# Attention and gated feed-forward on one core: 159 instead of 153 key blocks on VectorE, 12 more homes for hidden tiles, row chains interleaved, a new order

## The chip, the core and the metric

The kernel runs on one core of a Trainium2 chip. The core has five engines that run their own instruction queues in order and meet through semaphores: TensorE (PE, matmuls; its weight loads are listed apart as PEld), VectorE (DVE), ScalarE (ACT), GpSimd (POOL) and SyncE (SP), which here issues nearly all DMAs. Matmuls write to PSUM (eight banks of 128 partitions x 512 floats); everything else lives in SBUF. The metric is device time in microseconds of one execution; lower is better.

## The reference, cut to what matters

One input x of 2048 rows and 512 columns is normalised and goes into two branches whose results are added to x.

```python
xn = layernorm(x)                                   # 2048 x 512
# attention, 32 heads of 16
q, k, v = split(xn @ wqkv)                          # wqkv 512 x 1536
p = softmax(q @ k.T * 16 ** -0.5)                   # 32 x 2048 x 2048
a = (p @ v) @ wo
# gated feed-forward, 1792 hidden columns
gate, up = xn @ W_gate, xn @ W_up
h = where(gate > 0, gate, 0) * up
return x + a + h @ W_down
```

The exponentials are the large part: 32 x 2048 x 2048 of them.

## The kernel before, in words

**Attention.** The queries are cut into four blocks of 512 (c4 = 0 to 3), the heads into four groups of eight (gg), each group into two halves of four heads (ee). That makes 32 blocks in order of time; each goes over the 2048 keys in 16 key blocks of 128 (kt). For a key block and four heads, TensorE makes four score tiles of 128 keys x 512 queries. The array is cut into tiles of 64 rows x 32 columns: an operation uses one half of the 128 rows with four matmuls side by side, and the two halves work beside each other.

What happens to the scores is set by the table `QUAD_AT`, a line for each of the 32 blocks and a character for each key block:

- a dot: two units go to ScalarE. Each is one activation of 128 x 1024 (L1389) that reads two PSUM banks and writes exponentials to `ring`; there are two such pairs of banks, used in turn. Then one pair of value operations (8 matmuls) adds the key block's share to the block's output.
- a digit: the key block goes to VectorE, in `quad` (L1336). VectorE evicts each of the four score tiles with a bias as int16 (L1344, "d1"); read as bf16, these bits approximate the exponential. Two shifted copies of this pattern, `qa` and `qb`, with other shifts, even out the error. Each copy is made either by one VectorE instruction (L1363, 128 x 2048) or by two GpSimd instructions (L1359, 128 x 512 int32 each); bit 0 of the digit puts `qa` on GpSimd, bit 1 `qb`. All three patterns then go through the value matmuls: 3 x 8.

`QUAD_AT` has 153 digits before, so 359 key blocks and 718 activations are left to ScalarE. Four banks of pool `b` serve VectorE's scores, the value accumulations, the projections and the feed-forward in turn.

At the end of each block `normalise` evicts the output to `o_sb`, and takes the row sums through three small DMAs and a reciprocal (L1239) to `rb`; GpSimd multiplies (L1251, L1256). For the second half of the heads the result goes through `oT1` and four small DMAs (stream `pk`) into `oT`, which lies in `x_sb`.

**Feed-forward.** `glu(c4, ft)` (L1016) makes one hidden tile, 128 hidden columns x 512 rows: 16 matmuls for up, evicted by VectorE to `up_sb` (L1040), 16 for gate, and one VectorE instruction that gates and multiplies into a home in `hT` (L1044). There are 4 x 14 such tiles and `NHS` = 20 homes. Some tiles of the next query block are made together with this block's, to share a load of weights (`shared`).

**Rows.** `out_rows(c4, i)` (L1058) makes 128 output rows: a chain of 14 matmul pairs over the hidden tiles with `W_down` (in `Wd`, and in the homes of `Wk` and `Wv` when these are done), then four over the attention result with `wo`, and a VectorE addition of x (loaded into `xr_sb`, two slots) and a store. The rows of the last query block can't wait for its last heads: their first part is kept in fp32 in `xnT` (`resid(i)`, columns 0 to 1023 of part i, L1099) or, for two of them, stays in its bank. All matmuls of a chain are made to depend on all tiles of `reads`.

**The order.** The program makes a graph of 8248 operations, `Graph.op` collecting what each reads and writes. The order of all of them is not made when the program is built: it stands in the string `PLAN` as numbers, found beforehand by a search over a model of the engines, with the slot of each tile behind it. `Graph.run` reads it, adds the dependencies that come from the reuse of slots, and `Graph.emit` writes each engine's queue with the semaphore waits that are not already implied. The list `seq` gives the feed-forward's tiles and rows their places in the graph: all tiles of a query block, then its four row chains. `Pool` objects hand out the slots (`P_h` those of hidden tiles).

Of the kernel before, what the change touches and what calls it, by code (L numbers as in the profile page):

```python
# [14 lines left out]
ALU = mybir.AluOpType  # L15
# [28 lines left out]
ROW_AT = 20  # L44
XBANKS = (0, 1, 2, 3)
# [40 lines left out]
    "3...3..3..2..3..",  # L86
    "2...2..3..0..3..",
    "2...3..3..2..3..",
    "2...3..3..2..3..",
# [4 lines left out]
    "2...3..3..2..3..",  # L94
    "2...3..3..0..3..",
    "2...3..3..2..3..",
# [25 lines left out]
PLAN_OPS = 8248  # L122
PLAN = (
    "c-m!K1z;3M7v67n?{Wzd96~7)9Euky#fn1{v}hoK;8KbdcXx*Z#UWUc1S{?yij?ARg%p<nA>8f!Z)SJzHvEN<&E4+Ilka`+dvmFxr2dbKFK%6lf2^OxpPcvTGN*FSxG*2!#(Uzg@iI@fAXj{^<+x8@"
    "%6)Si-}BZZIh1?Wi;8boZof|$L0|XHm3{A9SJrLzy}8dF<9#T;*NnG~=Zyz+<6X!r<1XE12mQnqv4Rfy92EJAaiv>UfZpcj3mo26tqZQ$U$U%#_ciYGN&bQHBUf~J#l2=5&xoHaJB&+R@m)eUmxgY6"
    "1Mf<TVy*7=RX$=o=v_jrEyKoj@vvM?guuAZe1Kaql;**5!dTnG<bKeNI7+LmDA0wmjtHuEL0$U9ZE&$8Qryc8bEQY-YT!n=#1=+S<f4Xo@?W{UVg>|8pbR&RMXi6VU8KqKRjx=k#ie36ubayl(KlZZ"
    "Hkp@Zm}T5xJ)_w0XF*%xKB#iV=avr+x@m*ulCD_6H(%v;1K@*@uf*hc-3Kr$F6MW|ECM5~#yipxX1ho6K#?I4w=!QwxG%ZBoN;c4Gq+cx`6k)JEI2SPpBQc_9_EqpWxi+|cG5G(8XkzOFxxIx2)WG;"
    "v#>-|tRzVEh^;*em;WkE095*CSm<HqH|`M|cr09qT?N{VqVkBF%{%E!F2OyVSrjJo#C@^#5)-#ki(ELx!R42&{H1*&2Hxz52r$buahFFFHO%CC#9Q)JX4)?UB?Bn-@h~$EIv~rA8_Cs;WrYXK$Nit2"
    "M!^`XNhfIu!$pr-LS8yEID~)F1h<%6rs(#5!hPxRm9Y^lkGYG%5gr*R0~OLCGBU+!z=V64=^WYo$tfJMfyPTKzOG}v;bF$wOvcRc*~FY;Bv>(tiF*u~8(XJvKX15AfN<jhZuJo_&2ULV6kSIO6u07Z"
    "n^5&Yev|jYSj=N$RJvkR9J6dQw^K}4WnknQ2KJbTo4lwq%O)-%r<f?UuuDHk&%DjiSK&Se(yeb+R>Tduswg~lX?yeb(aF4Nkg+hqF8uHqwZ!ZoHmb)Pd?OPS5BUuDmX8s2!)cF~_zloVDiYqnivk~q"  # L130
    "nY1CwOy{3m@(zy-tptie8y<@zOv?m=nS1CyhNEu=B`7eOk-4-{f*<_M5>EDG7OrJlj3<qH<B}A0Uq6ShIT>w0_7VdV7WXDQb<H4KFK}%NhI8+iw?X?D-P<nA;$d8|bq!xzx2@%?Juea2d0J6Ycihz4"
    "iKpttb}qMXVl_42%G{@Q45=jhvlSWL=1(da;oV)g$rSi7X|g-_={ghMqMLJ*p}1~7rOW*c)nvS?_#*193-N&Jm2bY<vBgpM1wl8Rg-!aJs>hOTHhssvVvX}uy4D`TRBeJ=Dnik}C}X4+x2a?83x)z8"
    "P7M7D-$pVbhF-Mp(9NeUoO!Rm(9_&TEIgIe=U=4H*8F8n=~jp=p$ePY^|cgh5n-d%d3{m#82#JSWxiUqOr$1lsdSSV4fZs9w5f$mrt#t2l1_2~v;V<-Ua~WEtC}S<>(DK_7H`2Y3_dto2=#_e`(*Vt"
    "g9R+@W;o|D>5$AY83nqH+ATj!ijo4rE1_gF@^%OKB%gf8QYqHkoEu9rL-W|xonmNwAueE>v%JypMjKYVr8c%?2{)Cy)N9<j!4?E=hFLc`6E;RMR`D1WWsO<B25P)&-fH?P6*#ko0@_pi<kkdX=$0AY"
    "b-5+Vm{;o?c`)6VVKthH$2WqAMUB=5`+#hhw3ZGx!(`SvynFdD{aNE?a4o!<6(z;2ck1!(p?il87~_pKDf!TwTKRHY?HQuc1c<PXTbt^pKioTXnWmT_=C;>JnKGs*-f6>xf;lFcv!dN{GbE;9x6M>u"
    "tGxmi+^fa8t?L>ypru?bvh&uSabXVK-jem|O>Rzxu+2K$8f>l3FN?r5-n!Fl)?9I`7NeRin;X0Yo9|xdypb~dl5M=V+J(jQTxUwEcI)dZ+$){!Ga*kcp}qZ)f7yfok84w%BYZKC*;~J_!F>T9pD$Lg"
    "wKR=+qeb4{Dc*a8A$73TabdB#?_Tq~fZmp;6JjBm8p}iYu<YymJXI&NkD1(em|@|J+X7_G_r|e=PXlpp!?%=(#HU<JN3zp?4wWi>+}2KQ8>O0Xl~f(sUZ(aVEw7$1k1xLH;Kqe{xT0`h;%p~f+y@f="
    "#p_;p@l;sh|G&hSV$NGd7UwJG5s<F|7}p*}VZKms-w?tjWty|PhuKd*OpyhXdll~h=qn<#3DUrn>{8^QZP1{H!?fBMj-cq?QyE3E23c=Ev+<-S)iIUHH1ypZowzl}*=oWjam0RH`z&R)mpDwI*-m<l"
    "-F07|Ft;`PiA9;#$$+)7uNRn3de2=9BdmiRk7BV6Yy}`&q(#PxSMb=*&x}+UozfUkpjaJ1w?-jDoZ4;U)~S*uq%4Y&t;FXmw^OfTQ-I1BptV7t`zB_<CwadlFOM}``;H!TQ?!_AHAhZ!d{$sJG>=UO"
    "d1G(1JfA4^wjMd;d86r_>22g_Vaiy^I@dFhV5&6Ejjp4Z+@^aMF;t8<-d594yhLR-ck95_cb;iKjx_V)v%mzJUGsU*?d;;frr#{In(EdXI=L}cf7WRB=e`4Acp1*BBi%UrvQE+zZg1!O|IYQTpS{dx"  # L140
    "$|c2ys{fY|+}6kKyz0d?-RgE28MgEzPu+w6uRGfN0k;H!ZxG?BdGL$7?I$6yW7*dV?1#Dh3u@)c7oS1c(QXGk=cxuQ+j&6h-r^gM6#U;x*8FCdAKuy4dLFh;>zmGX?)#j=D_LNDBBJ|t@SUU^D|oNG"
    "M@eQ@eZ#68w``rwHXEfvi<LiPH*@+_yo0?-A76~WHm_}JMuA-z!_p~&aCK4lrdEM9=c{hTMrZa<ldK$CM^8M}NNqn`u~d7itaI<-d#ZGCdp^DL$d(S9+jf{4kHI>%GGj?J$jx(H&OFv==beibWBj$w"
    "78R@SS;vST>oWzj$$7kEnRwbf@3So{=Ky95OXf)@^Du9dvMExXS<|k0<X}IAlAVehW?Lud<{+jh7R`IfT(=$E8T`X+XIOfwdXXSEWS_y&1}vCIM1iOJ>_oTb3-hBKZYg`8#b$f-wtZ`&P<-0ME;qcN"
    "W?8gsJ#CF~)`xSjv$|!Ki4?1)n`5H)Lm1hi%mXT)q~c!=S2k+09pR?_e1xYyd9&$m`-j1)`nmT5Q!hmM7jusHsZ>W%itn>jbJnr5lwFbXR39v*5(Zx?Z`((whHU3H;p`pAQk}(k&-)al+T16Uzxcc&"
    "RfzZ(AKAh7nJ)KDNvYgVb!h87$m7PG<dye!D)1ho=wEzNXdB<`r}MtHl4=^TO)p;6<^2>uNeu~KRCV||_LpmkzZsDFzXwh@Kfi|x##s@lx~l4@OK6(^Csp@P!L#(5pL!pe@iZ&^#O;|ikDrJBIxmN5"
    "HyIw}rPmy8`iIeXaYL}@CCkXz)iBM;{=sc}|0W6mIT%9TF{GhwRDQm6LOGnKJ#hi`S>=^LuFA(Mvz@dGeWyQ22CA=YyP#~k7n$CqnbBT%{vHFAOSuPp9hmHNyRHGnpJhl1czXvZ@+yt?%5lBqEqc@K"
    "@_R-$`0WU;wk3kD(v2yNW0SWbxDXIBDo1;b7GB<w?bB-Q9d#?VO&GuTs1t4fJ`RoPZvgPB*F*%hUk^NU?IE`537o-SWpLtorXIj=Ps8zN+UJ=nlmRZTja;7+{Vi~5Y3r40x)<%XeXmzN98`{cN^-j0"
    "fu(`{F5Suacfe8S^3L<yulNl(wMc8P4gG2hurmG8JuJLbLm*xomQu&X;_m{dn{NBjHD;vVzeC}x6wC2>@8r@So!kn<J)Xg@6mqj))2D1m*$32$)E&z^YR$--<((F{UF=7%#r{*^W`WB^)n9=rxgPDQ"
    "F$@^z!spLh&jO=dZ*wFEJR1U(Y>?tmH#HqWacd6enr7=R0b|ywiw~4apw}i8|0^YJlC~U($=(JN-4uw6IC5O?5kC!R<Qj;_tJ^PH2Q(dosa@yM#i(sl`-DB99ZKc8l^^L6{ssoejoj}(hq;xHhVQ6^"
    "_5pg|S+BPP37FY?QgYyj1fXJ)BYg^Rfc%(<&jVNH1S(I%uS3T#j`HgrA#VMU2H#w!2$TX^6=9d%MP>qZS7G_}f_d(=7<26m(DGjP$!Okc4p1W4ec74QbrSd!{oSsj4VwVRdydASi3GN%(=P%CS<j0o"  # L150
    "qTL6w)EqZzLh0SQs^94KFA(XcPe$L*<VWkzepAqE7K&c}2FC}vV`HG6Am~QB%XaR1QsDYv?@RkPd<^>Ncj7jXv(%C@IFk`*=y)IU-v1AvKKx>v&Fn*oeTeSgM<OYN(9`)Ckl3u<!gZ}xk%K6#Vy#gU"
    "I1&1jn=L^UW&8*l)zuDGIZBsR9xyB!`rrEMp{s#r&*D(54m(AV>8qbYI$+wI?(-cnYbag$_xa&Tb2r(Mh;lKpQOjfIQSmve&VC$#`hSwjiNJwgJ5cBMN<iMFXup&%Kl%L-jQ<@d_z8Y*6AAG74x!Sm"
    "uL*G&F^+oEi2YR#CL$9D=Jv+qq2q^AEk6l-h#U`5n2O?7*0d=RJ0I+-yQgywAonsP^`ugKg3E1cj2+gZLqW=9w!GJztl_!Rny2R8gwsHUuP0-G`!3aI*um=Bvh5Q^S~t6!<HC*RC9@JVSsU(PwD@j("
# [408 lines left out]
def bass_parallel_sum__mha_block__glu_gated_reglu__prompt_kernel(  # L562
# [14 lines left out]
    with ExitStack() as es:  # L577
# [60 lines left out]

# [198 lines left out]

        chains = [0]

        def mm_chain(tile, pairs, reads, prio, sub=0, slots=None, mode="half", weights=None, flags=None):  # L840

            n = len(pairs)
            count = [0, n * (2 if mode == "half" else 1)]
# [598 lines left out]
```

## Time and profile before

| | us |
|---|---|
| median of 3 runs | 684.28 |
| lowest and highest | 684.1 and 685.0 |
| the profiled execution | 685.31 |
| its span, first to last instruction | 683.5 |

One execution is profiled. The page's first part gives, for each engine, the busy time, its share of the span and the number of instructions. The part on the chain follows the work that ended last back from its end, and says which engine and line each step is put down to. The groups list, for one source line and kind of instruction, the form out<-in, the count, after the bar the busy time and the mean duration of one in ns, and after the second bar the engine's idle time just before them and what ended it. All matmuls with cut tiles come from one helper (L255), so they are told apart by what they read: `ps<-qT,kT` are scores, `ps<-qd,v_aug` and `ps<-ring,v_aug` the value matmuls of VectorE's and ScalarE's key blocks. The windows give the same engines for a stretch from A to B microseconds. The timeline merges like instructions that follow each other: start, length, and their count. The granted TensorE clock was 1.00 in the steady part.

### The profile page before, as it was taken

To read this page: it belongs to the slowest core of one execution; us is meant where nothing else is said; L and a number is where in the kernel's file an instruction comes from. 1 tells how busy PE (TensorE), PEld (TensorE's weight loads), DVE (VectorE), ACT (ScalarE), POOL (GpSimd) and SP (SyncE) were. 2 spreads that over 40 slices of the span, in tenths; PEclk is the share of its full clock that TensorE was granted. 3 is DMA by queue.
4 is the path that set the end of the run, shared out by engine and by line. 5 is a ranking of instruction groups with operands and counts; after the bars stand their busy time and mean duration, and the time that the engine had idled before them with its cause. 6 is when DMAs were issued, how large, how long until landed. Compare 5 with 4: busy or idle time off the path is not lost.

```text
span 683.5 us, 44919 instructions
## 1 busy us (share of the span) xinstructions
PE 674.9 (99%) x22262; PEld 344.2 (50%) x19654; DVE 598.7 (88%) x1012; ACT 666.9 (98%) x730; POOL 499.4 (73%) x507
## 2 busy tenths in 40 slices
PE   8999999999999999999999999999999999999997
PEld 4455454546455555554444454544544445555543
DVE  9958899999989788999999788989998887988875
ACT  6999999999999999999999999999999999999994
POOL 3323768688788778887587886888878868778781
PEclk9999999999999999999999999999999999999999
DMA  7330120113122021212101022120111012131011
GB/s 216 58 73 14 53 82 27 30 53 97 56 66 64 6 73 38 70 40 63 35 23 31 17 70 66 39 66 7 55 40 52 22 51 71 40 93 32 25 32 55
DMA packets 55940, 35.86 MB, mean 52 GB/s; under 512 B 19336, under 2 KB 51784, under 8 KB 55752
## 3 DMA queue, kind: packets, MB, share of 16 engines
q1 hardware_dynamic: 55464, 32.71, 17.3%
q8 instruction: 164, 2.69, 1.6%
q10 hardware_dynamic: 288, 0.26, 0.1%
q14 instruction: 24, 0.20, 0.1%
HBM read 26.35 MB, written 2.35 MB: 42 GB/s over the span
## 4 chain that ended last, share of the span: by engine, by line
PE 71%; ACT 22%; DVE 4%; DMA 1%; issue 0%; POOL 0%; SPq 0%; ACTq 0%; DVEq 0%
PE ps L255 71%; ACT ring L1389 22%; DVE stats L750 1%; DVE qd L1344 1%; DMA xr_sb<-in_A_x_dram 1%; DVE xn_sb L763 1%; DMA rec_scr<-rrec 0%; DVE v_aug L900 0%; DMA x_sb<-in_A_x_dram 0%; DVE qT L976 0%; DVE mv L751 0%; ACT xn_sb L1188 0%; DVE xnT L804 0%; POOL rstd L745 0%; DVE xnT L1099 0%
## 5 line engine op out<-in xcount | busy, mean ns | idle before, releaser
L1389 ACT ACTIVATE ring<-ps 128x1024 bf16<-128x1024 f32 x718 | 660.5, 1143 | 1.8 <-PE ps L255 1.5
L1359 POOL TENSOR_TENSOR qd<-qd,ints 128x512 int32<-128x512 int32 x446 | 450.0, 1039 | 143.1 <-DVE qd L1363 72.6
L255 PE MATMUL ps<-qT,kT 64*32 64x512 bf16 x8192 | 448.0, 374 | 1.5 <-DVE xnT L1099 0.7
L1344 DVE TENSOR_SCALAR qd<-ps 128x512 int16<-128x512 f32 x612 | 396.7, 685 | 51.1 <-PE ps L255 48.0
L255 PE MATMUL ps<-qd,v_aug 64*32 64x512 bf16 x3672 | 262.3, 375 | 0.5 <-issue 0.4
L255 PE MATMUL ps<-ring,v_aug 64*32 64x512 bf16 x2872 | 236.7, 374 | 0.2
L1324 PEld LDWEIGHTS <-kT 64*32 64x32 bf16 x7584 | 150.1, 92 | 128.1 <-issue 34.7
L1296 PEld LDWEIGHTS <-v_aug 64*32 64x32 bf16 x4544 | 108.0, 91 | 72.6 <-issue 20.4
L255 PE MATMUL ps<-xnT,wgs 64*32 64x512 bf16 x1792 | 137.5, 374 | 0.0
L255 PE MATMUL ps<-xnT,wus 64*32 64x512 bf16 x1792 | 136.5, 375 | 0.0
L255 PE MATMUL ps<-Wd,hT 64*32 64x512 bf16 x768 | 58.9, 375 | 0.0
L834 PEld LDWEIGHTS <-wgs 64*32 64x32 bf16 x1792 | 43.0, 91 | 30.9 <-issue 6.8
L834 PEld LDWEIGHTS <-wus 64*32 64x32 bf16 x1792 | 43.1, 91 | 30.4 <-issue 7.6
L1363 DVE TENSOR_SCALAR qd<-qd 128x2048 int16<-128x2048 int16 x83 | 56.1, 690 | 2.3 <-PE ps L255 2.1
L834 PEld LDWEIGHTS <-hT 64*32 64x32 bf16 x1792 | 40.1, 92 | 29.5 <-issue 4.6
L255 PE MATMUL ps<-Wv,hT 64*32 64x512 bf16 x512 | 45.7, 375 | 0.0
L255 PE MATMUL ps<-Wk,hT 64*32 64x512 bf16 x512 | 42.7, 375 | 0.5 <-DVE qd L1344 0.3
L1044 DVE SCALAR_TENSOR_TENSOR hT<-ps,up_sb 128x512 bf16<-128x512 f32 x56 | 38.4, 685 | 4.2 <-PE ps L255 3.7
L1040 DVE COPY up_sb<-ps 128x512 f32<-128x512 f32 x56 | 38.4, 685 | 3.0 <-PE ps L255 2.4
L255 PE MATMUL ps<-Wo_p,x_sb 64*32 64x512 bf16 x480 | 40.0, 375 | 0.0
L255 PE MATMUL ps<-xnT,Wq 64*32 64x512 bf16 x480 | 36.4, 374 | 0.0
L255 PE MATMUL ps<-xnT,Wk 64*32 64x512 bf16 x480 | 35.1, 374 | 0.3 <-DVE xnT L804 0.3
(70 smaller groups left out, 264.4 us busy)
## 6 DMA issues: line engine op xcount, KB each, us to landing
rb<-rec_scr SPq DMA_DIRECT2D x31, 256.0 KB
wus<-in_B_W_up_dram SPq DMA_DIRECT2D x38, 128.0 KB, 2.9
wgs<-in_B_W_gate_dram SPq DMA_DIRECT2D x38, 128.0 KB, 2.9
xr_sb<-in_A_x_dram SPq DMA_DIRECT2D x16, 128.0 KB, 2.9
qT<-qf SPq DMA_DIRECT2D x120, 16.0 KB, 2.7
out_dram<-xn_sb SPq DMA_DIRECT2D x14, 128.0 KB, 2.5
x_sb<-in_A_x_dram SPq DMA_DIRECT2D x8, 128.0 KB, 2.4
x_sb<-oT SPq DMA_DIRECT2D x60, 16.0 KB, 2.7
```

The source lines that it names most:

```text
L255: return e.add_instruction(mybir.InstMatmult(name=e.bass.get_next_instruction_name(), engine=mybir.EngineType.PE, ins=[e.lower_ap(x), e.lo ...
L750: G.op("DVE", 580, lambda e, m=m: e.bn_stats(stats[:, m, :], xs(m)), reads=[t_xm[m]], writes=[t_st], prio=pr, order=last_xn if m == 4 else ())
L763: G.op("DVE", 320, lambda e, m=m, t=t_n: e.tensor_scalar(xn_sb[:, t.slot, :], xs(m), mv[:, m, 0:1], rstd[:, m:m + 1], op0=ALU.subtract, op ...
L834: e.ldweights(w()[rows, 32 * j:32 * j + 32], tile_position=(rows.start, 32 * j))
L1040: G.op("DVE", 603, lambda e: e.tensor_copy(up_sb[:, tup.slot, :], bank_of(tu)), reads=[tu], writes=[tup], prio=-590)
L1044: G.op("DVE", 603, lambda e: e.scalar_tensor_tensor(out=hT[:, th.slot, :], in0=bank_of(tg), scalar=0.0, in1=up_sb[:, tup.slot, :], op0=ALU ...
L1296: e.ldweights(vs(j), tile_position=(64 * half, 32 * j))
L1324: e.ldweights(ks(m), tile_position=(64 * half, 32 * m))
L1344: G.op("DVE", 601, lambda e, j=j, tx=tx: e.tensor_scalar(qd[:, tq.slot, 512 * j:512 * j + 512], ps[:, BANK[tx.slot], :], IBIAS[3], 0.0, op ...
L1359: G.op("POOL", POOL_NS / POOL_PIECES + 60, lambda e, x=x, n=n, c=slice(i * m, i * m + m): e.tensor_tensor(x().bitcast(I32)[:, c], raw().bi ...
L1363: G.op("DVE", 600, lambda e, n=n, x=x: e.tensor_scalar(x(), raw(), float(SHIFTS[n + 1]), None, op0=ALU.add), reads=[ti, tq], writes=[t], p ...
L1389: exp_ops[u] = G.op("ACT", 904, lambda e, tr=tr, k0=k0: e.activation(ring[:, tr.slot, :, :], ps[:, 4 * k0:4 * k0 + 2, :], ACTF.Exp, scale= ...
```

## The change

Six characters of `QUAD_AT` go from a dot to 2, one in each of six blocks (numbers 10, 12, 18, 21, 26 and 28, counted from 0):

```diff
-    "2...3..3..2..3..",
+    "2.2.3..3..2..3..",
...
-    "3...3..3..2..3..",
+    "3.2.3..3..2..3..",
```

A hidden tile may lie in one of 12 more homes: the 512-column parts of `xnT` that belong to query blocks already done. Where the last query block keeps its rows in `xnT`, only those homes are allowed that its `resid` doesn't need early:

```diff
-        P_h = Pool("h", NHS)
+        P_h = Pool("h", NHS + 12)
...
+        def h_of(t):
+
+            if t.slot < NHS:
+                return hT[:, t.slot, :]
+            a, dt = divmod(t.slot - NHS, 4)
+            return xnT[:, dt, 512 * a:512 * a + 512]
...
-            th = t_h[(c4, ft)] = Tile("h", P_h)
+            th = t_h[(c4, ft)] = Tile("h", P_h, list(range(NHS)) + [NHS + 4 * a + dt for a in range(c4) for dt in range(4)
+                                                               if c4 < NB - 1 or a == 2 or dt in TAIL_ACT])
...
-                out=hT[:, th.slot, :], in0=bank_of(tg), scalar=0.0, in1=up_sb[:, tup.slot, :], op0=ALU.max, op1=ALU.mult),
+                out=h_of(th), in0=bank_of(tg), scalar=0.0, in1=up_sb[:, tup.slot, :], op0=ALU.max, op1=ALU.mult),
...
-                         reads=[t, txr], writes=[tr] + (t_xnT if i == 0 else []), prio=p1)
+                         reads=[t, txr], writes=[tr] + (t_xnT if i == 0 else []) + [Tile("res%d" % a, P_h, [NHS + 4 * a + i]) for a in range(2)], prio=p1)
+                resids.append(o)
...
+        for a in range(3):
+            guard = Tile("xnT")
+            guard.r.extend(o for o in t_xnT[a].w + t_xnT[a].r if o not in resids)
+            P_h.cur[NHS + 4 * a:NHS + 4 * a + 4] = [guard] * 4
```

In a row chain each pair of matmuls depends on its own hidden tile and its own part of `W_down` or `wo`, instead of on all of them:

```diff
-                    G.op("PE", 216, fn, reads=reads, joins=[tile],
+                    need = reads[i] if each else reads
+                    G.op("PE", 216, fn, reads=need, joins=[tile],
...
-                reads += [t_h[(c4, ft)] for ft in range(FT)] + [t_wd]
                 for ft in range(FT):
-                    pairs.append(((lambda th=t_h[(c4, ft)]: hT[:, th.slot, 128 * i:128 * i + 128]), (lambda ft=ft: wd_of(ft))))
+                    reads.append([t_h[(c4, ft)], only(t_wd, ft)])
+                    pairs.append(((lambda th=t_h[(c4, ft)]: h_of(th)[:, 128 * i:128 * i + 128]), (lambda ft=ft: wd_of(ft))))
...
-                reads.append(to)
+                reads.append([to, only(t_wo, g)])
```

The four row chains of a query block no longer stand behind all its tiles, but between the tiles of the next one, with `ROW_STEP[c4]` tiles (0, 1, 2, 2) ahead of each:

```diff
+            step = ROW_STEP[c4]
+            for n, row in enumerate(behind):
+                seq += tiles[n * step:n * step + step] + [row]
+            seq += tiles[len(behind) * step:]
+            behind = rows
+        seq += behind
```

The `pk` copies use four streams for each of their four places instead of two (`(n // 2) % NGG`). And the whole string `PLAN` is another one: 8302 operations instead of 8248, the order searched again with a model in which the array's two halves take the time that they take in traces. The 54 more are the six key blocks': each has 17 operations on VectorE's way and 8 on ScalarE's.

More of the change, by code (lines that the diff above doesn't have):

```diff
@@ L44 @@
 ROW_AT = 20
+ROW_STEP = (0, 1, 2, 2)
 XBANKS = (0, 1, 2, 3)
@@ L93 @@
     "2...3..3..0..3..",
-    "2...3..3..2..3..",
+    "2.2.3..3..2..3..",
     "2...3..3..0..3..",
-    "2...3..3..2..3..",
+    "2.2.3..3..2..3..",
     "2...3..3..0..3..",
@@ L838, in bass_parallel_sum__mha_block__glu_gated_reglu__prompt_kernel, with mm_chain @@
         chains = [0]
-        def mm_chain(tile, pairs, reads, prio, sub=0, slots=None, mode="half", weights=None, flags=None):
+        def mm_chain(tile, pairs, reads, prio, sub=0, slots=None, mode="half", weights=None, flags=None, each=False):
             n = len(pairs)
@@ L1056, in resid, with only @@
             return xnT[:, i, 0:1024].bitcast(FP32)
+        def only(t, n):
+            part = Tile()
+            part.w.append(t.w[n])
+            return part
         def out_rows(c4, i, gs, first, last, slots=None, pr=0.0, tile=None, sub=0):
```

224 lines of the change are left out of this document (115 added, 109 removed).

## The prediction

> **What bounds the kernel now.** I read the page first: engine shares and the chain that ended last. Then I read ScalarE's stretches in order of time, and last the windows, to see which engine's rate stays fixed while the others' varies.
>
> ```profile
> span 683.5 us, 44919 instructions
> ...
> PE 674.9 (99%) x22262; PEld 344.2 (50%) x19654; DVE 598.7 (88%) x1012; ACT 666.9 (98%) x730; POOL 499.4 (73%) x507
> ...
> PE 71%; ACT 22%; DVE 4%; DMA 1%; issue 0%; POOL 0%; SPq 0%; ACTq 0%; DVEq 0%
> ...
> L1389 ACT ACTIVATE ring<-ps 128x1024 bf16<-128x1024 f32 x718 | 660.5, 1143 | 1.8 <-PE ps L255 1.5
> ```
>
> Two engines look full, PE (99%) and ACT (98%), and the chain is put down to PE for 71%. That alone doesn't decide: PE's busy time is modelled. ACT's row is clearer: 718 exponentials, and only 1.8 us idle before all of them. In order of time (start, length, count; each length reaches to the end of the last one, 1.14 us after its start):
>
> ```profile
> 10.99 2.87 ACT L1389 ACTIVATE ring<-ps 128x1024 bf16<-128x1024 f32 x3
> ...
> 126.58 21.19 ACT L1389 ACTIVATE ring<-ps 128x1024 bf16<-128x1024 f32 x23
> 146.53 14.08 ACT L1389 ACTIVATE ring<-ps 128x1024 bf16<-128x1024 f32 x15
> 160.77 5.61 ACT L1389 ACTIVATE ring<-ps 128x1024 bf16<-128x1024 f32 x6 [0.17 <-PE ps L255]
> 165.31 21.24 ACT L1389 ACTIVATE ring<-ps 128x1024 bf16<-128x1024 f32 x23
> ...
> 651.34 2.94 ACT L1389 ACTIVATE ring<-ps 128x1024 bf16<-128x1024 f32 x3
> 652.24 2.04 ACT L1389 ACTIVATE ring<-ps 128x1024 bf16<-128x1024 f32 x2
> 654.70 16.76 ACT L1389 ACTIVATE ring<-ps 128x1024 bf16<-128x1024 f32 x18 [0.42 <-PE ps L255]
> ...
> 663.05 10.25 ACT L1389 ACTIVATE ring<-ps 128x1024 bf16<-128x1024 f32 x11
> ```
>
> Three readings. The rows at 651.34 and 652.24 are one stretch asked from two points, so they give two neighbouring starts: **0.90 us** apart, the closest that ACT runs. From the first start, 10.99, to the last, 663.05+10.25-1.14 = 672.16, there are 717 spacings: 661.2/717 = **0.922 us** on average, 2.4% above the closest. And the head (11.0 us) and tail (10.2 us after the last exponential ends) are small. Now the windows:
>
> ```profile
> 400.00:450.00 50.00, 50.00 (x1776) 25.97 (x1536) 44.80 (x73) 50.00 (x55) 40.11 (x40) 1.00 0.21 58
> ...
> 500.00:550.00 50.00, 49.63 (x1572) 22.00 (x1336) 43.28 (x72) 50.00 (x55) 38.96 (x38) 1.00 0.12 33
> ...
> 11.00:673.30 662.30, 659.43 (x21971) 337.04 (x19382) 585.40 (x969) 660.46 (x719) 493.20 (x492) 1.00 0.18 50
> ...
> 227.70:247.70 20.00, 20.00 (x720) 10.92 (x612) 15.58 (x26) 20.00 (x23) 15.25 (x16) 1.00 0.09 25
> ```
>
> The columns are length, then busy time and count of PE, weight loads, DVE, ACT, POOL. Two windows of 50 us hold 1776 and 1572 matmuls, 13% apart, and the same 55 exponentials. The engine whose count doesn't move sets the pace: **ACT**. PE's "99%" contains matmuls that stand ready and wait; 227.7 to 247.7 shows it can do 720 in 20.0 us, 36.0 a microsecond, against 21971/662.3 = 33.2 on average. PE ends the small delays (0.922 against 0.90), not the bulk.
>
> **The change, part by part.** (a) Six key blocks of 128 keys leave ACT for VectorE. Each takes two exponentials off ACT: 12 x 0.922 = **11.06 us** less. By the closest spacing it would be 12 x 0.90 = 10.8.
>
> (b) What six blocks add:
>
> ```profile
> L1359 POOL TENSOR_TENSOR qd<-qd,ints 128x512 int32<-128x512 int32 x446 | 450.0, 1039 | 143.1 <-DVE qd L1363 72.6
> L1344 DVE TENSOR_SCALAR qd<-ps 128x512 int16<-128x512 f32 x612 | 396.7, 685 | 51.1 <-PE ps L255 48.0
> L255 PE MATMUL ps<-qd,v_aug 64*32 64x512 bf16 x3672 | 262.3, 375 | 0.5 <-issue 0.4
> L255 PE MATMUL ps<-ring,v_aug 64*32 64x512 bf16 x2872 | 236.7, 374 | 0.2
> ...
> L1363 DVE TENSOR_SCALAR qd<-qd 128x2048 int16<-128x2048 int16 x83 | 56.1, 690 | 2.3 <-PE ps L255 2.1
> ```
>
> All six carry the mark 2: the pattern qa by one DVE instruction, qb by two of POOL. DVE: four evictions at 396.7/612 = 0.648 and one at 56.1/83 = 0.676, so 3.27 us a block, **19.6 us** in all. POOL: two at 450.0/446 = 1.009, 2.02 a block, **12.1 us**. PE: 3672/153 = 24 value matmuls for a VectorE block, 2872/359 = 8 for an ACT one, scores alike: 16 more a block, 96 in all, 96/33.2 = **2.9 us** if the array were the bound. It has to do 22067 in 662.3-11.06 = 651.2 us, 33.9 a microsecond, below the 36.0 it has shown; so nothing.
>
> (c) Whether DVE and POOL can take it. Counting the exponentials in order (two for each key block left on ACT) puts the six in the 20 us pieces that begin at 227.7, 268.5, 389.7, 450.2, 551.2 and 591.4.
>
> ```profile
> 166.20:186.30 20.10, 20.10 (x680) 10.49 (x584) 19.90 (x34) 20.10 (x24) 14.95 (x15) 1.00 0.18 53
> ...
> 186.30:652.20 465.90, 464.51 (x15560) 236.69 (x13614) 411.06 (x670) 465.03 (x507) 372.62 (x365) 1.00 0.17 47
> ...
> 268.50:308.80 40.30, 40.30 (x1380) 20.22 (x1196) 37.95 (x63) 40.30 (x46) 34.80 (x35) 1.00 0.18 51
> 450.20:490.50 40.30, 40.30 (x1324) 19.78 (x1180) 36.71 (x60) 40.30 (x46) 34.61 (x35) 1.00 0.14 40
> ```
>
> DVE's densest piece has 34 instructions in 20.10 us, 0.591 each, with ACT undisturbed. The long stretch would hold 670+30 in 465.9-11.06 us, 0.650 each: room on average. Not everywhere: 268.5 to 308.8 would hold 63+5 in 40.3-1.84 = 38.5 us, 0.566 each, 1.7 us too much; 450.2 to 490.5 comes to 0.592, just full. POOL there: (34.80+2.02)/38.5 = 96%. So three DVE instructions have to leave the piece at 268.5. The next part allows it.
>
> (d) Homes and interleaving move the feed-forward work; they add no instruction. A hidden tile may lie in a finished 512-column part of xnT, and row chains stand between tiles, so tiles (two DVE instructions each, L1040 and L1044) can run in pieces like 227.7 to 247.7, where DVE is busy 15.58 of 20.0 us. Same L1044, same weight loads, no DMA of its own. The added wait: L1044 waits for the last reader of its xnT part, L1099 for the readers of homes it overwrites. Behind them on DVE stand the evictions L1344, for them the scores on PE, then ACT. I take 0; bounds: a gain of one wait like the next, to a loss of the 1.7 us if no tile can move.
>
> (e) Row chains move with their loads of xr (one 128 KB DMA each); on SP's queue they stand among the weight loads and the normalisation's DMAs.
>
> ```profile
> 648.11 4.62 DMA xr_sb<-in_A_x_dram
> ```
>
> Such a load, late in the chain, lands at 652.73, and ACT's 652.24 to 654.70 is two spacings, 2.46 instead of 1.84 us: **0.62 us** for one such event. Sixteen rows could cost 9.9 at worst, or give back 0.6; spread wider, they press less on the two xr slots, so 0. The waits per matmul pair instead of per chain let a chain start before its last hidden tile; the split of the pk streams lets 60 small copies go without waiting for an earlier user. Both only loosen: 0, between -0.6 and +0.6. Cover: ACT's buffered scores.
>
> (f) The nearest row for a piece with six VectorE blocks is one that the kernel already has. From 126.58 to 146.53 are 22 spacings, 19.95 us (five blocks, 0.907 each). From 146.53 to 165.31 are 20, 18.78 us (six, 0.939), with a wait on PE in it. Against 20 x 0.922 = 18.44 that is 0.34 more. I charge it six times: **2.04 us**. Ends: 0, and twice that.
>
> Sum: -11.06 + 2.04 = **-9.0 us**. The profiled execution took 685.31 (span 683.5 and 1.8 around it), so 676.3; it lay 1.0 above the median of 684.28, which becomes **675.3**.
>
> **Rivals.** *The array is the bound (slower).* The chain's 71% speaks for it, the two 50 us windows against. From 36.0 matmuls a microsecond on it decides. Price +2.9: 687.2. Chance 0.03.
>
> *VectorE's work lands on the path.* If tiles don't move away, evictions come late, PE's queue stands in order behind the score that needs the bank, and ACT starves. Half of 30 x 0.591 = 17.7 on the path: -11.06+8.9, 682.1, chance 0.08. All of it: +6.7, 690.9, chance 0.04; it decides where a piece asks for less than 0.591 us an instruction. For it speaks the piece at 268.5; against it, that DVE waited 48.0 us for PE before L1344.
>
> *POOL is late (slower).* POOL already waited 72.6 us for L1363. Each new L1363 can hold it 0.69 us on top of 2.02: 6 x 2.71 = 16.3, less 11.06: +5.2, 689.5, if all is on the path; from a POOL share near 100% on. Without that hold it would be 12.1 less 11.06: +1.1, 685.4. Chance of the first 0.03. [...]
>
> *The new order also repairs the small delays.* If it came halfway from 0.922 to the 0.907 of the good piece: 705 x 0.9145 = 644.7 instead of 661.2, -16.5: 667.8. Against it: shares of DVE and PE rise. Chance 0.13.
>
> *The order doesn't fit the chip*: new waits eat the gain, 684 within 1.4. Chance 0.05.
>
> **How the numbers follow.** Forecast 0.64, its own range 671.9 (-11.06 and two events of 0.62 gone) to 679.0 (twice 2.04 and the 1.7 charged). The range reaches to the nearer part of the repaired order and of the half-hidden VectorE: 668.0 to 682.5, leaving about 2 in 10 out. Faster: 0.64+0.13+0.08 = 0.85; same 0.05; slower 0.10. 0.2%, 1.4 us, is about what a measurement of this kernel can tell from no change.
>
> **What would show it.** ACT with 706 exponentials, first to last start near 652 us (0.925 each), idle still under 3 us: right. DVE near 618 us busy, POOL near 511. Pieces at 227.7, 389.7 and 551.2 with hidden tiles where there were none: (d) right. Spacings well over 0.94 with DVE near full in the piece that now begins at about 268: the VectorE rival. POOL near 100% there: the POOL rival. Mean spacing under 0.917: the repaired order. The forecast is wrong if ACT's spacing doesn't stay between 0.91 and 0.93, or head and tail change by over 2 us.

## The result, and the profile after

| | before | after |
|---|---|---|
| time, median of 6 runs each, side by side (us) | 685.07 | **681.36** (679.98 to 682.63) |
| ratio to before, with its 95% interval | 1 | **0.9946** (0.9929 to 0.9962) |
| time of the profiled execution, its span (us) | 685.31, 683.5 | 681.0, 678.1 |
| TensorE's instructions: matmuls + weight loads | 22262 + 19654 = 41916 | 22358 + 21562 = 43920 |

The forecast was 675.3 us, a gain of 9.0. The gain was 3.7 us, and in two later batches the same kernel stood at 1.0014 and 1.0018 of the kernel before, which is no gain. So the question is where 5 to 10 us went.

The page of the kernel after (busy time, share and count of each engine; a queue's packets, megabytes and share; the chain; groups of instructions with count, busy time, mean ns, and the idle time before them):

```profile
span 678.1 us, 46986 instructions
...
PE 668.2 (99%) x22358; PEld 392.7 (58%) x21562; DVE 615.1 (91%) x1042; ACT 657.9 (97%) x718; POOL 511.7 (75%) x519
...
q8 instruction: 171, 2.80, 1.7%
...
PE 91%; DVE 5%; DMA 2%; POOL 1%; issue 0%; SPq 0%; ACT 0%; DVEq 0%; POOLq 0%
...
L1418 ACT ACTIVATE ring<-ps 128x1024 bf16<-128x1024 f32 x706 | 651.4, 1079 | 6.2 <-PE ps L263 5.3
...
L1373 DVE TENSOR_SCALAR qd<-ps 128x512 int16<-128x512 f32 x636 | 412.3, 684 | 36.2 <-PE ps L263 32.3
...
L1353 PEld LDWEIGHTS <-kT 64*32 64x32 bf16 x8032 | 170.9, 92 | 101.7 <-issue 15.5
L1325 PEld LDWEIGHTS <-v_aug 64*32 64x32 bf16 x6004 | 144.8, 92 | 71.8 <-issue 11.2
```

The rows of the page before that the prediction did not use, for the same things:

```profile
q8 instruction: 164, 2.69, 1.6%
...
L1324 PEld LDWEIGHTS <-kT 64*32 64x32 bf16 x7584 | 150.1, 92 | 128.1 <-issue 34.7
L1296 PEld LDWEIGHTS <-v_aug 64*32 64x32 bf16 x4544 | 108.0, 91 | 72.6 <-issue 20.4
```

The twelve exponentials are gone (706 for 718), and ACT's busy time on them fell by 9.1 us (660.5 to 651.4). But ACT's idle time rose from 1.8 to 6.2 us, nearly all of it waiting for TensorE's scores, and the chain is now TensorE's for 91%. The row that should have been read against the forecast is the weight loads': **1908 more** (448 of kT, 1460 of v_aug), for 96 more matmuls. The program leaves a load out when the operation ahead of it in its half of the array uses the same weights. The new order stands such operations apart. The two q8 rows (packets, megabytes, share), of the queue of kind "instruction", go with TensorE's count: 2.80 MB / 43920 and 2.69 MB / 41916 are both about 64 bytes, and there is one packet for 43920/171 = 257 and 41916/164 = 256 of TensorE's instructions, one every 4 us (678.1/171).

Where the time went can be seen at three kinds of places.

**One stall behind SyncE's queue.** ACT's timeline after (start, length, count, and in brackets the idle time ahead with what ended it):

```profile
284.35 6.53 ACT L1418 ACTIVATE ring<-ps 128x1024 bf16<-128x1024 f32 x7
292.85 3.85 ACT L1418 ACTIVATE ring<-ps 128x1024 bf16<-128x1024 f32 x4 [1.98 <-PE ps L263]
...
568.19 7.48 ACT L1418 ACTIVATE ring<-ps 128x1024 bf16<-128x1024 f32 x8 [0.38 <-PE ps L263]
```

VectorE's timeline there:

```profile
288.28 0.68 DVE L1373 TENSOR_SCALAR qd<-ps 128x512 int16<-128x512 f32 x1
291.10 0.25 DVE L1268 RECIPROCAL rrec<-rsum 128x16 f32<-128x16 f32 x1 [2.14 <-DMA rsum<-o_sb]
291.27 1.82 DVE L1373 TENSOR_SCALAR qd<-ps 128x512 int16<-128x512 f32 x3
```

And SyncE's, where a row is the issue of a DMA:

```profile
282.45 0.47 SPq L1269 DMA_DIRECT2D rec_scr<-rrec  x1
285.21 0.58 SPq L1272 DMA_DIRECT2D rb<-rec_scr  x1
285.84 0.47 SPq L1118 DMA_DIRECT2D out_dram<-xn_sb  x1
286.35 0.59 SPq L1267 DMA_DIRECT2D rsum<-o_sb  x1
```

Read from the bottom up: the copy of the row sums goes out at 286.35, behind the rb copy, which had waited from 282.92 to 285.21 for its own input. The row sums had been evicted to `o_sb`, from where this copy takes them, since 276.6. The reciprocal stands at the head of VectorE's queue until 291.10, the evictions behind it stand too, then TensorE has no bank for the next score, then ACT misses 1.98 us.

**VectorE full.** The window 370 to 392 of the kernel after, then of the kernel before (length, busy time and count of PE, weight loads, DVE, ACT, POOL):

```profile
370.00:392.00 22.00, 22.00 (x764) 14.12 (x716) 21.51 (x36) 20.80 (x24) 18.44 (x19) 1.00 0.15 42
```

```profile
370.00:392.00 22.00, 21.83 (x700) 9.92 (x600) 17.51 (x29) 21.90 (x25) 18.14 (x19) 1.00 0.05 12
```

VectorE is busy 21.51 of 22.0 us, and ACT loses 1.2 (22.0 - 20.80) where it lost 0.1 before.

**TensorE late with no wait open.** Its timeline after, near 567 us, then the weight loads':

```profile
566.46 0.38 PE L263 MATMUL ps<-ring,v_aug 64*32 64x512 bf16 x4
566.68 0.38 PE L263 MATMUL ps<-qT,kT 64*32 64x512 bf16 x1
567.34 0.38 PE L263 MATMUL ps<-qT,kT 64*32 64x512 bf16 x3 [0.28 <-issue]
```

```profile
566.46 0.10 PEld L1353 LDWEIGHTS <-kT 64*32 64x32 bf16 x4
567.35 0.09 PEld L842 LDWEIGHTS <-Wq 64*32 64x32 bf16 x4 [0.79 <-issue]
```

One score is four matmuls on the same finished input. The first starts at 566.68, the other three 0.66 us later, though no wait that falls between them was still open; no load starts in that time either, and the idle time is put down to "issue". ACT misses 0.38 us for it, the last row of its timeline above. Such places can be counted over the whole trace. For each operation I took the latest of: the end of all that its waits name (those that the program places inside the operation ahead of it too), the start of the one ahead in its half plus 0.2155 us (the usual pitch), and the start of the one ahead in the queue. An operation over 0.3 us later than that is called **late** below. Before has 5 (2.3 us in all), after 8 (3.9 us). All eight start 1.1 to 1.65 us after a q8 packet ended, a band that by chance would hold one in seven.

Their place in TensorE's queue says more. I also took the waits from the times at which the semaphores reach their values, and found by this second rule 7 late operations in the kernel after and 13, 17, 18 and 21 in numbers 5, 8, 10 and 13 below, 76 together. When TensorE's instructions are counted in their order, 72 of these 76 begin 194 to 202 past a multiple of 256; by chance it would be 3. That is the spacing of the q8 packets too, one for 256 or 257 of TensorE's instructions. So the late operations go with the packets in time and in place; what holds TensorE up there no row shows.

### The profile page after: what moved, and what is told of

Same layout as the page of the kernel before. It is cut to its first block, busy times and chain, and to the rows that moved or that the text cites. A ratio compares the mean times of both kernels' runs of the same rounds, so it can differ in the third digit from the quotient of the medians.

```text
span 678.1 us, 46986 instructions
## 1 busy us (share of the span) xinstructions
PE 668.2 (99%) x22358; PEld 392.7 (58%) x21562; DVE 615.1 (91%) x1042; ACT 657.9 (97%) x718; POOL 511.7 (75%) x519
## 4 chain that ended last, share of the span: by engine, by line
PE 91%; DVE 5%; DMA 2%; POOL 1%; issue 0%; SPq 0%; ACT 0%; DVEq 0%; POOLq 0%
PE ps L263 91%; DVE qd L1373 1%; DVE stats L758 1%; DVE xn_sb L771 1%; DMA rsum<-o_sb 1%; DMA xnT<-xn_sb 1%; POOL qd L1388 0%; DVE v_aug L909 0%; DMA rec_scr<-rrec 0%; DMA x_sb<-in_A_x_dram 0%; DVE qd L1392 0%; DVE qT L985 0%; DVE kT L902 0%; DVE mv L759 0%; DVE xnT L812 0%
## 5 line engine op out<-in xcount | busy, mean ns | idle before, releaser
L1418 ACT ACTIVATE ring<-ps 128x1024 bf16<-128x1024 f32 x706 | 651.4, 1079 | 6.2 <-PE ps L263 5.3
L1388 POOL TENSOR_TENSOR qd<-qd,ints 128x512 int32<-128x512 int32 x458 | 462.0, 1039 | 131.3 <-DVE qd L1392 81.0
L263 PE MATMUL ps<-qT,kT 64*32 64x512 bf16 x8192 | 466.6, 374 | 3.5 <-DVE qd L1373 2.4
L1373 DVE TENSOR_SCALAR qd<-ps 128x512 int16<-128x512 f32 x636 | 412.3, 684 | 36.2 <-PE ps L263 32.3
L263 PE MATMUL ps<-qd,v_aug 64*32 64x512 bf16 x3816 | 310.3, 375 | 0.1
L263 PE MATMUL ps<-ring,v_aug 64*32 64x512 bf16 x2824 | 244.2, 375 | 0.0
L1353 PEld LDWEIGHTS <-kT 64*32 64x32 bf16 x8032 | 170.9, 92 | 101.7 <-issue 15.5
L1325 PEld LDWEIGHTS <-v_aug 64*32 64x32 bf16 x6004 | 144.8, 92 | 71.8 <-issue 11.2
L263 PE MATMUL ps<-Wv,xnT 64*32 64x512 bf16 x576 | 36.7, 374 | 0.5 <-DVE v_aug L909 0.3
L263 PE MATMUL ps<-Wk,hT 64*32 64x512 bf16 x384 | 35.8, 375 | 0.0
```

Source lines behind the costliest of these rows:

```text
L263: return e.add_instruction(mybir.InstMatmult(name=e.bass.get_next_instruction_name(), engine=mybir.EngineType.PE, ins=[e.lower_ap(x), e.lo ...
L1325: e.ldweights(vs(j), tile_position=(64 * half, 32 * j))
L1353: e.ldweights(ks(m), tile_position=(64 * half, 32 * m))
L1373: G.op("DVE", 601, lambda e, j=j, tx=tx: e.tensor_scalar(qd[:, tq.slot, 512 * j:512 * j + 512], ps[:, BANK[tx.slot], :], IBIAS[3], 0.0, op ...
L1388: G.op("POOL", POOL_NS / POOL_PIECES + 60, lambda e, x=x, n=n, c=slice(i * m, i * m + m): e.tensor_tensor(x().bitcast(I32)[:, c], raw().bi ...
L1418: exp_ops[u] = G.op("ACT", 904, lambda e, tr=tr, k0=k0: e.activation(ring[:, tr.slot, :, :], ps[:, 4 * k0:4 * k0 + 2, :], ACTF.Exp, scale= ...
```

## The experiments

Each batch ran on another chip, with the kernel before beside it: 686.33 us in the first batch, then 686.05, 686.06 and 686.70. Runs are compared within their batch. "The six blocks" are those in which the change moves a key block to VectorE.

**1. ACT released alone, in the old order** (the kernel before).

```diff
+            w = 8 if blocks.index(key[:3]) in SIX and key[3] == 2 else 512
-            ... e.activation(ring[:, tr.slot, :, :], ps[:, 4 * k0:4 * k0 + 2, :], ...
+            ... e.activation(ring[:, tr.slot, :, 0:w], ps[:, 4 * k0:4 * k0 + 2, 0:w], ...
```

> The kernel before, with the 12 exponentials of the six key blocks cut from 2 x 512 to 2 x 8 columns (the rest of their ring tiles is left out); nothing is added anywhere and the order is the old one. It measures what the release of ScalarE alone is worth. If ScalarE sets the pace, as the prediction had it: 10 to 11.5 us under the kernel before. If VectorE and the array are as late as ScalarE in those places: 3 to 7 us. If only the array counts: under 2 us.

Measured 685.38 us, 0.999 (0.9977 to 1.0002). Twelve nearly empty exponentials are worth nothing where they are. Waits of ACT (us, times, longest):

```profile
ACT ring L1391 <- PE ps L256: 9.4, 17, 0.9
```

That is 1.5 us in the kernel before: most of what ACT no longer computes it waits for scores, since the other queues keep their order. In the old order, then, a term like (a) is not paid out.

**2. VectorE loaded alone** (the kernel before, 24 more statistics instructions, 13.2 us by the page's busy time, ahead of evictions of the six blocks).

```diff
+                    if o.name == "d1":
+                        o.fn = lambda e, fn=o.fn, spot=spots.pop(0): (e.bn_stats(spot, Wq[:, 0, :]), fn(e))[1]
```

> The kernel before, with 24 more VectorE instructions (a statistics instruction over 128 x 512 bf16, about 0.59 us each, 14 us in all, results unused), one ahead of each of the four evictions of one VectorE key block in each of the six blocks. Nothing is taken off ScalarE. If VectorE has room, as the prediction had it: 0 to 1.5 us over the kernel before. If its work lands on the path: 4 us and more, up to 14.

Measured 696.76, 1.0144 (1.0126 to 1.0163): 10.4 us for 13.2. In the old order VectorE has hardly any slack at these places either, so 0 to 1.5 us was the wrong expectation.

**3. The added VectorE and GpSimd work taken away** (the kernel after).

```diff
+            few = blocks.index(key[:3]) in SIX and key[3] == 2
+            wd, wq, wp = (8, 32, 16) if few else (512, 2048, 1024 // POOL_PIECES)
```

> The changed kernel, with the six added key blocks' VectorE and GpSimd instructions cut to 8 of 512 columns (24 evictions and 6 patterns on VectorE, 12 on GpSimd); matmuls and order unchanged. If VectorE's (or GpSimd's) added work is what ate the gain: 4 to 7 us under the changed kernel, so 674 to 677. If the loss is the array's or lies in single waits of the new order: within 1.5 us of it, 680 to 682.

**4. The 96 added matmuls cut to 8 columns** (the kernel after).

```diff
+                w = 8 if narrow else 512
-                        ... ps[32 * j:32 * j + 32, BANK[t.slot], :], vs(j), src[j](rows), ...
+                        ... ps[32 * j:32 * j + 32, BANK[t.slot], 0:w], vs(j), src[j](rows)[:, 0:w], ...
```

> The changed kernel, with the 96 added value matmuls (patterns qa and qb of the six added key blocks) cut from 512 to 8 columns. If the array sets the pace: about 2.5 us under the changed kernel, 679. If VectorE or ScalarE does: within 1 us of it.

**5. The kernel after again**, as the measure for the second batch.

> The changed kernel, unaltered, on the chip of the three below. Stalls in which TensorE waits for nothing but its own instructions come and go between executions; if they are what makes it vary, its ratio here lies anywhere from 0.993 to 1.003, and the profile shows more of them than that of the kernel before (about 2.3 us there). If not, 0.993 to 0.996 as before.

Number 3 measured 687.50, 1.0004 (0.9985 to 1.0024), number 4 687.17, 1.0014 (0.9997 to 1.0032), number 5 686.88, 1.0014 (0.9998 to 1.0030). The unaltered kernel stood one batch later, on another chip, where the lightened ones stand. So taking the work of the 30 + 12 instructions of VectorE and GpSimd, or that of the 96 matmuls, away brings nothing back that can be measured. By number 1, work taken out of a fixed order need not show, so this says that they aren't what binds as the rest stands, not that they cost nothing.

**6. The row sums' copy six places earlier in SyncE's queue** (the kernel after, whole computation).

```diff
+        late = [t for t in queued if ops[t].stream == ("n1", 3)][2]
+        turns.remove(late)
+        turns.insert(turns.index(queued[queued.index(late) - 6]), late)
```

> The changed kernel, with one DMA (the row sums of block 11) six places earlier in SyncE's queue, so that it goes before a wait for another block's landing. Its late landing held VectorE 2.1 us near 290 us. If that stall is part of what ate the gain: 1.5 to 2.5 us under the changed kernel in the same call, and the exponentials' 2 us gap there gone. If the time is lost again behind it: within 0.5 us.

Measured 684.98, 0.9986 (0.9966 to 1.0006), 1.9 us below number 5 (from the scatter of the two, an interval of about 0.2 to 3.3). SyncE's timeline has the copy out at 279.53, and ACT's has no wait left there:

```profile
279.53 0.56 SPq L1274 DMA_DIRECT2D rsum<-o_sb  x1
```

```profile
279.05 19.84 ACT L1425 ACTIVATE ring<-ps 128x1024 bf16<-128x1024 f32 x21
```

**7. Fewer weight loads** (the kernel after; 1784 of them left out).

```diff
-            elif held[o.half] == o.wkey:
+            elif o.wkey in held[o.half]:
                 o.load, o.wsrc = False, ()
...
-                held[o.half] = o.wkey
+                held[o.half] = held[o.half][-2:] + [o.wkey]
```

> The changed kernel, with 1784 of its 21444 weight loads left out (those whose weights stood in the same half at most three loads ago; their matmuls then use another tile's weights), so that TensorE has as many instructions as in the kernel before. Order and matmuls unchanged. If the longer instruction stream starves TensorE: 3 to 6 us under the changed kernel in the same call, and its unexplained late starts fall to about 2 us. If not: within 1 us.

Measured 679.44, 0.9919 (0.9896 to 0.9942): **7.4 us** below number 5 by the medians (6.6 by the means, with an interval of about 4.9 to 8.2), some 4 ns for each load. Number 5 has 14 late operations (8.9 us in all, every one in that band behind a packet), this one 4 (2.2 us): they fall by 6.7 us, about as much as the time. ACT's waits for scores (us, times, longest), in number 5, then here:

```profile
ACT ring L1418 <- PE ps L263: 8.4, 17, 1.9
```

```profile
ACT ring L1420 <- PE ps L263: 5.0, 9, 1.4
```

**8. More weight loads** (the kernel before; the 2608 loads that it skips are made, whole computation).

```diff
-            elif held[o.half] == o.wkey:
-                o.load, o.wsrc = False, ()
-            else:
-                held[o.half] = o.wkey
```

> The kernel before, with 2608 more weight loads (every matmul operation loads its weights, also where they stand in the array already); results unchanged. If the number of TensorE's instructions matters: 3 to 8 us over the kernel before, with more of the unexplained late starts. If loads are hidden and fetched in time: within 1 us.

Measured 695.91, 1.0155 (1.0128 to 1.0181): **9.9 us** above the kernel before, 3.8 ns for each. 16 operations are late (8.5 us). An operation still follows the one ahead in its half by 0.215 us in the median, as in the kernel before, so the added loads don't lengthen the array's usual pitch. The direction holds both ways. What about a load costs time, its work or its being an instruction? The next batch begins with its measure.

**9. The kernel after once more**, for the third batch (`a_same` in the texts below).

> The kernel after, unaltered, as the measure for the other three of this batch, which run on the same chip. Every theory: between 0.994 and 1.002 of the kernel before, as its two earlier measurements gave (0.9946 and 1.0014).

Measured 686.37, 1.0018 (0.9996 to 1.0039).

**10. The array's work taken away, every instruction kept** (the kernel after).

```diff
+                    w = 8 if src_eng and st[0] else 512
-                        ... ps[32 * j:32 * j + 32, BANK[t.slot], :], vs(j), src[j](rows), ...
+                        ... ps[32 * j:32 * j + 32, BANK[t.slot], 0:w], vs(j), src[j](rows)[:, 0:w], ...
```

> The kernel after, where every value matmul of a pattern (qd with v_aug, 3816 matmuls or 954 operations) except the first of each accumulation computes 8 columns instead of 512, so the rest of its product is left out. The instructions, their number and their order stay. At the pitch of one operation in each half (0.2155 us) that takes about 954 x 0.2155 / 2 = 103 us of work off the array. Theory 1 (TensorE is held up by the number of its instructions, each of which has to be brought in): within 2 us of a_same, as nothing is taken out of the stream. Theory 2 (the added weight loads cost work of the array itself): with 103 us of it free, at least as much below a_same as the run with 1784 loads left out was below its own unaltered kernel, 7.4 us.

Measured 688.02, 1.0017 (0.9990 to 1.0043): no better than number 9. The page, the group that was narrowed, and a place in TensorE's timeline:

```profile
PE 663.5 (97%) x22355; PEld 361.2 (53%) x21562; DVE 615.6 (90%) x1042; ACT 659.0 (96%) x718; POOL 511.5 (74%) x519
```

```profile
L263 PE MATMUL ps<-qd,v_aug 64*32 64x8 bf16 x3748 | 123.1, 164 | 0.5 <-PE ps L263 0.2
```

```profile
545.62 0.38 PE L263 MATMUL ps<-ring,v_aug 64*32 64x512 bf16 x3
545.69 0.38 PE L263 MATMUL ps<-qT,kT 64*32 64x512 bf16 x4
546.71 0.37 PE L263 MATMUL ps<-ring,v_aug 64*32 64x512 bf16 x1 [0.64 <-issue]
```

3748 matmuls compute 8 columns, 101 us of the array's work are gone (937 operations at 0.2155 us in two halves), and the page still calls PE 97% busy. A narrowed operation really frees its half: the next one there starts 0.05 us behind it in the median, not 0.215. The fourth matmul of an operation stands a whole microsecond behind its third. There are 19 late operations here, 11.1 us in all, 17 of them in the band behind a packet. The columns that the array multiplies are not what the kernel lacks time for.

**11. Both mends together** (the kernel after, the edits of 6 and 7).

> The kernel after with both mends: 1784 weight loads left out (those whose weights were among the last three of their half; those products are made with the wrong weights) and the row sums' copy of the block with the stall issued six places earlier in SyncE's queue. If the two causes are separate, their effects add: 7.4 + 1.9 = 9.3 us below a_same, 0.986 to 0.990 of the kernel before, which is the -9.0 us of the prediction. If they are one delay seen twice, it is no lower than 7.4 us below a_same.

Measured 678.57, **0.9887** (0.9864 to 0.9910), 7.8 us below number 9 and 7.5 below the kernel before. The forecast's ratio, 675.3/684.28 = 0.9869, lies in that interval. Whether the two effects add fully (9.3) isn't settled by it. It is a measure of causes and no kernel to use, as its products are made with wrong weights.

**12. Fewer loads with the right weights** (the kernel after with the edit of 6; in the planned order 229 value operations moved by hand beside one with the same v_aug weights, 139 of them forward; 932 loads fall away).

```diff
-PLAN = (order of the kernel after)
+PLAN = (the same, 139 value operations earlier and 90 later)
```

> The kernel after with the whole computation, the same row-sum copy six places earlier, and TensorE's order altered: 229 value operations are moved next to an earlier or later operation of the same array half that uses the same v_aug weights, so that 932 of 21444 weight loads fall away, with right weights everywhere. Theory 1: 932 x 4 ns = 3.7 us, and 1.9 us by the copy, 5.6 us below a_same, less what the moved operations disturb: 2 to 5.6 us below. If only the change of order counts (rival: the planner's order is good as it is, and any hand move makes new waits): at or above a_same less 1.9 us.

Measured 696.20, 1.0153 (1.0130 to 1.0176): slower by 10, a miss. It has few late operations (2, 0.9 us), but ACT's waits are many and short:

```profile
ACT ring L1425 <- PE ps L263: 8.8, 29, 0.7
```

That is only 1.4 us more than in number 9 (7.4, 16 times), so it doesn't account for the 10 us. That an operation brought forward pushes the scores behind it back, and with them ACT, would fit, but no run shows it. Number 15 moves none forward.

**13. As many instructions, but no loads** (the kernel before, whole computation).

```diff
+                cols = ((0, 504), (504, 512)) if kt % 16 in TWICE else ((0, 512),)
                 for m in range(4):
-                    ins = matmul_loaded(e, ps[32 * m:32 * m + 32, bank(), :], ks(m), ...
+                    for a, b in cols:
+                        ins = matmul_loaded(e, ps[32 * m:32 * m + 32, bank(), a:b], ks(m), ...
```

> The kernel before, whole computation, no weight load added: in 5 of every 16 key tiles each score matmul of 512 columns is made as one of 504 and one of 8, so 2560 matmul instructions more for the same columns. Theory 1a (what counts is the number of TensorE's instructions, whatever they are): like the 2608 added weight loads, which cost 9.9 us: 7 to 12 us above the kernel before. Theory 1b (it is the weight loads as such, by their own time in the array or ahead of it): within 2 us of the kernel before.

Measured 698.06, 1.0161 (1.0139 to 1.0182): **11.4 us** above the kernel before. The page:

```profile
PE 684.5 (98%) x24822; PEld 344.7 (49%) x19654; DVE 601.1 (86%) x1012; ACT 672.6 (96%) x730; POOL 499.5 (72%) x507
...
q8 instruction: 174, 2.85, 1.8%
```

The loads are those of before; the matmuls are 2560 more. 24 operations are late, by 11.5 us in all, and 22 of them start 1.1 to 1.65 us after a q8 packet ended. A split score also keeps its half a little longer (0.240 us to the next start in the median, against 0.215), some 8 us in each half over the kernel, so the total alone would not decide; the late operations and number 10 do.

**14. Fewer loads in the old order** (the kernel before, the edit of 7; 1592 loads left out).

> The kernel before with 1592 of 19536 weight loads left out in the same way as in the kernel after (weights among the last three of their half; those products are made with the wrong weights). If the loads cost the same everywhere, 3.8 to 4.1 ns each: 6 to 6.5 us below the kernel before. If the delay begins only where the stream is denser than before's, as the few late starts in before's trace (five, 2.3 us together) suggest: 0 to 3 us below.

Measured 685.52, 0.9985 (0.9973 to 0.9996): 1.2 us for 1592 loads, 0.7 ns each, where the kernel after paid 4.1. From the density of the kernel before (41916/683.5 = 61.3 instructions a microsecond) downwards, taking an instruction out was worth 0.7 ns; from that of the kernel after (43917/684.2 = 64.2 in number 5), 4.1.

**15. Operations moved only to later places** (the kernel after with the edit of 6; the plan's order altered as in 12, for 127 value operations and only backwards; 516 loads fewer, whole computation).

> The kernel after, whole computation, the row-sum copy six places earlier, and 127 value operations moved only to a later place, next to the operation of the same half with the same v_aug weights; 516 of 21444 weight loads fall away and no score is pushed back. Theory: 516 x 4 ns + 1.9 us = 4 us below the unaltered kernel, which stood at 1.0014 and 1.0018 of the kernel before: 0.995 to 0.998. If any hand move of the order makes new waits, as in the run that also moved operations forward: above 1.002.

Measured 689.27, 1.0040 (1.0026 to 1.0054): a miss too, though far smaller than number 12. Five operations are late (2.4 us). Here too, moving by hand in a searched order cost more than these loads returned; why isn't shown. Number 6 is the fastest kernel with the whole computation in the later batches, and its interval does not part it from the kernel before.

In the table, 43920 and 43917 are the same program: three records are missing in the later traces.

| kernel | TensorE's instructions | late operations | us against before in its batch |
|---|---|---|---|
| 14, before with fewer loads | 40324 | 2 (0.8 us) | -1.2 |
| before | 41916 | 5 (2.3 us) | 0 |
| 7, after with fewer loads | 42133 | 4 (2.2 us) | -6.6 |
| 11, after with both mends | 42133 | 6 (3.9 us) | -7.5 |
| 12, after, moved both ways | 42985 | 2 (0.9 us) | +10.1 |
| 15, after, moved backwards | 43404 | 5 (2.4 us) | +2.6 |
| after, first measurement | 43920 | 8 (3.9 us) | -3.7 |
| 5, after, second batch | 43917 | 14 (8.9 us) | +0.8 |
| 9, after, third batch | 43917 | 15 (6.6 us) | +0.3 |
| 10, after, less work, all instructions | 43917 | 19 (11.1 us) | +2.0 |
| 13, before with split scores | 44476 | 24 (11.5 us) | +11.4 |
| 8, before with more loads | 44521 | 16 (8.5 us) | +9.9 |

Rows with more instructions have, by and large, more late operations; the time doesn't follow them in every row: number 12 is slow with hardly a late operation. By the second rule, numbers 3, 4 and 6 have 15 (7.8 us), 12 (6.1 us) and 11 (6.0 us).

## Why the forecast was wrong

**The step that failed is (b)'s price of TensorE.** It counted 96 matmuls, found 33.9 a microsecond below the 36.0 shown, and wrote "so nothing"; what the new `PLAN` does to the weight loads was counted in no part. "Same weight loads" in (d) speaks of the feed-forward and is right there (1792 each for up, gate and the hidden tiles, before and after); the 1908 more are attention's. The runs showed in its place: the array's work indeed isn't the bound (number 10), but the number of TensorE's instructions costs time, from about the density of the kernel before (61.3 a microsecond) upwards. The new order adds 2004 instructions, 1908 of them loads, because operations with the same weights no longer follow each other in a half. Taking 1784 of them out gives 7.4 us back; adding some 2600 instructions to the old order, of either kind, costs 10 to 11. In the later batches, where the whole gain of 9.0 was missing, that is most of it. In the first measurement 5.3 us were missing, and its trace shows a sum of smaller things: 1.6 us more in late operations than before, the stall of 2.0, and 1.1 where VectorE is full; no run takes them away on that chip. Why the same kernel had 3.9 us of late operations in its first profile and 8.9 and 6.6 in later ones, which goes with 0.9946 and then 1.0014 and 1.0018, stays open.

**What bounds the kernel.** "The engine whose count doesn't move sets the pace" made ACT the bound and set the chain of waits (PE 71%) aside. Number 1 shows how far that holds: twelve exponentials off ACT give nothing while the order stands. TensorE's 99% was rightly distrusted, since it is 97% even with 101 us of work out; but the conclusion that TensorE therefore has room did not follow. The sign on the page was the number of loads, 19654, then 21562. The loads' busy share, which rose from 50% to 58%, is no measure of it either: it is 49% in number 13, which is slow, and 53% in number 10, which is no faster than number 9.

**(a) and (f)** Right, and in place. Exponentials counted in order, two for each key block left on ACT, give the pieces of the six blocks in the trace after. They run 3.54 us above ACT's closest spacing, against 1.51 before; 2.0 us, as (f) charged. Together they last 111.9 us instead of 120.7: 8.8 less, where (a) and (f) give 9.0. The loss lies outside them: from the first exponential to the last it is 656.5 us instead of 661.1, so the other 26 blocks together became 4.2 us longer. By the prediction's own sign this is wrong: 0.931 us a spacing lies outside 0.91 to 0.93, and ACT's idle time is 6.2 and not under 3. With both mends of number 11 the time falls 7.5 us below the kernel before, of 9.0.

**(b), VectorE and GpSimd.** Right: POOL's busy time rose by 12.3 us (12.1 forecast), VectorE's by 16.4 for 19.6, of which the evictions' by 15.6 as forecast. Taking them away in number 3 changed nothing that can be measured.

**(c)** Right in kind, wrong in place: the stretch that is too full ends at 392, and ACT loses 1.2 us in the window shown (busy 20.80 of 22.0). No run altered it, so that VectorE is the cause there is read from the profile only. The piece feared most was relieved as (d) said that it could be: from 267.5 to 306.0 VectorE now has 56 instructions, where 63 stood and 68 were feared.

**(d)** Right in what it says of the tiles: the pieces that now begin at 228.1, 390.9 and 549.3 hold one, two and one hidden tile, where there were none.

**(e)** The second error. "Spread wider, they press less … so 0" weighed the row chains' loads; what fell behind in SyncE's queue was the row sums' copy of a normalisation, and by number 6 it cost 1.9 us. A loss of that size lies in the bounds of the step (0.6 back to 9.9 lost), but the value taken was 0, and the cause isn't the one weighed.

**The rivals.** The time measured first, 681.36, lies in the stated range (668.0 to 682.5; the forecast's own range begins at 672.0 by its terms, not at 671.9) and next to a rival's price, VectorE's work half on the path (682.1, chance 0.08). That is luck: number 3 takes this work away and nothing comes back. New waits that eat the gain (684 within 1.4, chance 0.05) fit the ratios of the later batches, but their mechanism was not named: that would have needed a count of the weight loads in the new order, which the diff doesn't print but the plan holds. The array as the bound is ruled out by number 10, and number 3 speaks against GpSimd.

## What to carry to other kernels

When an order of work is changed, count each engine's instructions in the new order, weight loads included, and not only the work that they do: two operations that share weights need one set of loads as neighbours and two apart, and taking 1784 loads out gave 7.4 us here. A "busy" share that is 99% and still 97% when 101 us of the work are taken out was no measure of room here. Late operations that no wait explains were the sign here (5 in the kernel before, 24 with 2560 more instructions); the page's total of idle time marked "issue" was not (ahead of the kT loads it fell from 34.7 to 15.5 us). And a searched order is hard to mend by hand, so the count has to be priced in the search.

## What the runs showed of the hardware

- The queue of kind "instruction" (q8) moved about 64 bytes for each of TensorE's instructions, and one packet for some 256 of them (2.69 MB and 164 packets for 41916, 2.85 MB and 174 for 44476). At 59 to 63 of TensorE's instructions a microsecond over the span (40324/683.2 = 59.0, 43404/686.0 = 63.3) 2 to 6 operations were late in a run; from 64 up (44476/697.3 = 63.8, 43920/678.1 = 64.8) 8 to 24 were, mostly by 0.3 to 1.3 us and 1.1 to 1.65 us behind the end of a packet. The kernel before had five (2.3 us), the kernel after 8 to 15 (3.9 to 8.9 us).
- When the first matmuls past 194 + 256 k in TensorE's order are laid in order beside the packets of the kernel after, from 17 us on, a packet starts 0.2 to 1.9 us (0.9 in the median) after the matmul at the place ahead, takes 1.05 us, and the matmul beside it never starts sooner than 1.3 us after its end. With the median start and length that is some 3.2 us of the 3.8 between two packets. The late ones of that trace had a packet that started 1.25 us or more behind (1.5 in the median); what held it back isn't shown, nor what ties the matmul to it.
- An instruction of TensorE's cost about 4 ns where it was taken out of the kernel after or added to the kernel before (7.4 us / 1784, 9.9 us / 2608, 11.4 us / 2560), and 0.7 ns where it was taken out of the kernel before (1.2 us / 1592), whether it loads weights or multiplies (with the reserve made for the split scores in number 13). These are differences between whole runs divided by a count, not the time of one instruction.
